# Second query block's maxima moved into the start stage, and x loaded ahead of the values' weights: an attention kernel on one core

## The chip, the core and the metric

The kernel runs on one core of a Trainium2 chip. The core has a matrix engine (TensorE, PE in the profile, with PEld for loading its stationary operand), VectorE (DVE), ScalarE (ACT), GpSimd (POOL), a sync engine (SP) that issues transfers, and 16 DMA engines. Work goes through on-chip memory: SBUF, and eight accumulation banks of 128 x 512 float32 (PSUM) into which TensorE writes. The metric is device time in microseconds (us) of one execution; lower is better.

## What is computed

Two attention layers of 32 heads with 20 features each read the same x (2048 x 640), and a gate mixes their outputs:

```python
def attn(x, wqkv, wo):            # once with A's weights, once with B's
    q, k, v = split(x @ wqkv)     # 32 heads of 20
    p = softmax(q @ k.T * 20 ** -0.5)
    return merge(p @ v) @ wo
g = sigmoid((x * gate_w).sum(-1, keepdims=True))
out = g * attn_A(x) + (1 - g) * attn_B(x)
```

All inputs and the output are float32.

## The kernel before

**Precision.** x and the weights are split in float16 pairs (high and low part), after scaling by a power of two that comes from the largest absolute value of the tensor. `scales` (L171) makes such powers for several tensors at once: a transpose of the column maxima on TensorE (L177), a reduction and some integer arithmetic on VectorE (L166 to L187), two tiny products that spread the result to all partitions (L194), and a copy (L197). It is a generator that marks with `PRODUCT` the places where TensorE is used. A projection takes three products per chunk of 128 features (high-high, high-low, low-high), so fifteen for 640 features.

**Tiling.** Heads go in groups of four (`g`, 16 groups over both layers), queries in blocks of 512 (`qb`, four), keys in chunks of 512 (`ch`, four) or tiles of 128. A step `G` of the main loop handles two key tiles of one (g, qb): eight score products (L670), eight exponentials on ScalarE (L673), two groups of value products accumulated in `acc` (L688), and, where one is due, a slice of a coming projection (L405). There are 512 steps, eight for each (g, qb).

**Row maxima.** Softmax needs the maximum of each query's scores before its exponentials. It is made in a pass of its own. A unit `u` of that pass is one query tile of 128 and two heads; eight units make one (g, qb). For each of the four key chunks and two heads, `max_mm` (L596) makes one product (L612) in a bank and evicts it. Plain eviction is a reduction on VectorE (L623). With `two`, chunks are taken in pairs: the first product uses the difference of two key chunks (tiles `KD`), ScalarE takes its relu into `rl` (L616), and VectorE adds the second chunk's product and reduces in one instruction (L620), which replaces one of two reductions by a relu. Before the change `two` holds for both pairs of chunks in block 0 (u < 8), for the first pair with both heads in the rest of group 0, and for the first pair of one head later. `finish_max` (L627) then brings the eight units' maxima through VectorE, GpSimd and a small round trip over DRAM (`m_scr`, L644 and L648, issued on SP) into extra rows of the queries' tile.

**Order.** It is written out by hand; every engine runs its own instructions in the order in which they are emitted, and waits in that order. `take` (L133) picks one of seven banks by the kernel's own clock estimate.

- The start stage (from L863): loads on SP, on ScalarE's and on GpSimd's queue; absolute maxima (`largest`); one chain of `scales` for five tensors; transposes of x (L900) with their splits on ScalarE and VectorE (L904, L905); projection of the first group's keys and some query features (`a_chunk`), of the remaining query features (`r_chunk`, L947), each spread to its rows by small DMAs on SP and GpSimd alternately (L451, L453); the key differences (`differences_of`, GpSimd, L496 to L500).
- The ramp (L990): for each half (chunk pair) and each of the eight units of block 0, four products of maxima, then `go_on` with the rest of the first projections (`rest`: three remainder chunks, then the sixteen tiles of the values' projection) for 1.3 us of the kernel's own clock. Then `finish_max` for block 0, with `rest` going on.
- The main loop (L1125 on): in each step `next_maxima` (L1114) hands out the coming units' chunks: four a step when the unit lies fourteen steps ahead, at 1.5 times that pace while it is nearer (`RAMP`), none when it would be fifteen or more ahead (`LEAD`).

Of the kernel before, what the change touches and what calls it, by code (L numbers as in the profile page):

```python
# [11 lines left out]
F32 = mybir.dt.float32  # L12
I32 = mybir.dt.int32
AF = mybir.ActivationFunctionType
OP = mybir.AluOpType
AX = mybir.AxisListType
# [3 lines left out]
P = 128  # L20
S = 2048
D = 640
# [32 lines left out]
        "X m0 m1 e0 m1 e0 e1 V e1 e0 m1 m0 V e1 m0 m1 m0 e0 e1 X")  # L55
LATE = "e0 e1 e0 e1 V X e0 e1 e0 e1 V"
RAMP = 1.5
BETWEEN = 1.3
NB = 7

T_SCORE, T_MODE, T_VALUES, T_READY = 0.217, 0.1, 0.85, 0.39
# [9 lines left out]
def kernel(  # L71
# [57 lines left out]
    block_end = [0.0, None]  # L129
    free_at, held = [0.0] * NB, set()  # L130
    now = [-1]

    def take():  # L133

# [19 lines left out]
    def tick_block(cost, ready=0.0):  # L154

        begin = block_end[0] if now[0] < 0 and block_end[1] == rows_free else max(rows_free) + T_MODE
        clock["pe"] = max(begin, ready)
        rows_free[:] = [clock["pe"] + cost + T_MODE] * 2
        block_end[:] = [clock["pe"] + cost, list(rows_free)]
        clock["done"] = clock["pe"] + cost + T_READY - T_MODE  # L160
# [10 lines left out]
    def scales(maxima, n, then):  # L171

        for _ in range(REST):
            yield
        yield PRODUCT
        i, pt = take()
        nc.tensor.transpose(pt[:n, :P], maxima[:, :n], ident)  # L177
        tick_block(0.1, free_at[i])
        yield
        e = wts.tile([5, 8], F32, name="e", tag="scl", bufs=2)  # L180
        nc.vector.tensor_reduce(e[:n, 0:1], pt[:n, :P], axis=AX.X, op=OP.max)
        give(i, spend("dve", 0.3, clock["done"]))
        spend("dve", 1.0)
        powers(e.bitcast(I32)[:n, :], 1)
        dg = wts.tile([5, 2, 5], F32, name="dg", tag="scd", bufs=2)
        for k in range(2):
            nc.vector.tensor_scalar(dg[:n, k, :n], ident[:n, :n], e[:n, 3 + k:4 + k], None, op0=OP.mult)  # L187
        for _ in range(REST):
            yield
        yield PRODUCT  # L190
        i, pb = take()
        tick_block(0.1, free_at[i])
        for k in range(2):
            nc.tensor.matmul(pb[:, k * n:(k + 1) * n], ones[:n, :], dg[:n, k, :n], start=True, stop=True)  # L194
        yield
        both = wts.tile([P, 10], F32, name="both", tag="scb", bufs=2)
        nc.vector.tensor_copy(both[:, :2 * n], pb[:, :2 * n])  # L197
        give(i, spend("dve", 0.2, clock["done"]))
        then(both[:, :n], both[:, n:2 * n])
# [56 lines left out]
    def largest(dst, src):  # L256
        nc.vector.tensor_reduce(dst, src, axis=AX.XY, op=OP.max,
                                apply_absolute_value=True)
        spend("dve", 0.5)
# [138 lines left out]
    def mms(i, out_ap, pairs, cost):  # L398

        if now[0] >= 0:  # L400
            tick_block(len(pairs) * cost * T_SCORE, free_at[i])
        for k, (a, b) in enumerate(pairs):
            if now[0] < 0:
                tick_block(cost * T_SCORE, free_at[i])
            nc.tensor.matmul(out_ap, a, b, start=(k == 0), stop=(k == len(pairs) - 1))  # L405
            if now[0] < 0:
                yield

    def turns(n):

# [32 lines left out]
    def run(gen):  # L443
        for _ in gen:
            pass
# [145 lines left out]

    def max_parts(g, qb):
        m = mparts[g, qb] = wts.tile([P, 2, 2, 4, 4], F32, name="mpart", tag="mpart", bufs=2)
        nc.gpsimd.memset(m[:, :, 0:1 if g else 2, :, 0] if g or qb else m, LOW)

    def max_mm(u, ch, heads=(0, 1)):  # L596

        g, qb, i = unit_of(u)
        pair, t = divmod(i, 4)
        if (g, qb) not in mparts:
            max_parts(g, qb)
        q0 = qb * QB + t * P
        for j in heads:
            two = u < NS or ch < 2 and (j == 0 or g == 0)
            i, pt = take()
            ready = tick_score(j, i)
            r = slice(64 * j, 64 * j + 60)  # L610
            k = KD[g % 2 if ch == 0 else 1][r, pair] if two and ch % 2 == 0 else KT[g % 2][r, pair, ch * QB:(ch + 1) * QB]
            nc.tensor.matmul(pt, QT[g % 2][r, pair, q0:q0 + P], k, start=True, stop=True)  # L612
            m = mparts[g, qb][:, pair, j, t, ch:ch + 1]
            if two and ch % 2 == 0:
                relus[u, j] = start.tile([P, QB], F32, name="rl0", bufs=4) if u < NS else work.tile([P, QB], F32, name="rl", bufs=2)
                nc.scalar.activation(relus[u, j], pt, AF.Relu)  # L616
                back = relu_at[u, j] = spend("act", T_EXP, ready)
            elif two:
                rl = relus.pop((u, j))
                nc.vector.tensor_tensor_reduce(rl, pt, rl, 1.0, LOW, OP.add, OP.max, m)  # L620
                back = spend("dve", T_MAX, max(ready, relu_at.pop((u, j))))
            else:
                nc.vector.tensor_reduce(m, pt, axis=AX.X, op=OP.max)  # L623
                back = spend("dve", T_MAX, ready)
            give(i, back)
# [244 lines left out]
    w_t = wqkv[0].rearrange("(c p) f -> p c f", p=P)  # L870
    for part in range(2):
        nc.sync.dma_start(ws[:, part], w_t[:, :, part * D:part * D + 320])
    nc.sync.dma_start(wv[:, :, :160], w_t[:, :, 2 * D:2 * D + 160])
    for i in range(0, NT, 2):
        nc.sync.dma_start(xs[:, i:i + 2, :], x_t[:, i:i + 2, :])
    nc.scalar.dma_start(wv[:, :, 160], gate_w.rearrange("(c p) -> p c", p=P))
    mrow = wts.tile([P, S], F16, name="mrow", tag="cq", bufs=2)[:4]
    nc.gpsimd.memset(mrow, MS)
    for i in range(2):
        for j in range(2):  # L880
            nc.gpsimd.dma_start(KT[i][64 * j + 60:64 * j + 64], mrow.unsqueeze(1).to_broadcast([4, 2, S]))
    for i in range(2):
        nc.gpsimd.memset(V[i][:, :, :, DH:VW], 1.0)
    xm = start.tile([P, 8], F32, name="xm")
    wm = start.tile([P, 5], F32, name="wm")
    for part in range(2):
        largest(wm[:, part:part + 1], ws[:, part])
    largest(wm[:, 2:3], wv[:, :, :160])
    largest(wm[:, 3:4], wv[:, :, 160:161])
    for i in range(8):  # L890
        largest(xm[:, i:i + 1], xs[:, 2 * i:2 * i + 2, :])
    nc.vector.tensor_reduce(wm[:, 4:5], xm, axis=AX.X, op=OP.max)

    def turn(j0, c):

# [13 lines left out]
    def turns_of(j0, cs=range(NC)):  # L909
        for c in cs:  # L910
            turn(j0, c)()
            yield

    max_parts(0, 0)
    load, split_next = weights_a(1)
    load()
    drains = [turn(0, c) for c in range(NC)] + [turn(4, 0)]
    found = []
    run(scales(wm, 5, lambda r, inv: found.extend((r, inv))))
    r, inv = found  # L920
    r_x = r[:, 4:5]
    hi, lo = blk["a", 0] = block_tiles("a")
    split_now(ws[:, 1, :, 0:GF], r[:, 1:2], hi[:, :, 0:GF], lo[:, :, 0:GF])
    split_now(ws[:, 0, :, 0:48], r[:, 0:1], hi[:, :, GF:P], lo[:, :, GF:P])
    for f in drains:
# [5 lines left out]
    nc.gpsimd.tensor_copy(hi.rearrange("p c (j f) -> p c j f", j=4), w_r)  # L931
    nc.gpsimd.tensor_tensor(lo.rearrange("p c (j f) -> p c j f", j=4), w_r, hi.rearrange("p c (j f) -> p c j f", j=4),
                            op=OP.subtract)
    nc.vector.tensor_copy(inv_x, inv[:, 4:5])
    halves = []
    both = cycle((nc.sync, nc.gpsimd))

    def a_chunk(ch):
        if ch % 2 == 0:
            halves.append(half_tiles(0))  # L940
        n = slice((ch % 2) * QB, (ch % 2 + 1) * QB)
        hl = halves[ch // 2][:, :, n]
        yield from project_chunk(blk["a", 0], hl[:, 0], hl[:, 1], ch)
        for pair in range(2):
            run(spread(0, hl, ch * QB, QB, q=(0,) if ch == pair == 0 else (), k=(pair,), queues=both))

    def r_chunk(ch, pairs):  # L947
        yield from project_r(0, ch)
        n = slice((ch % 2) * QB, (ch % 2 + 1) * QB)
        run(spread(0, halves[ch // 2][:, :, n], ch * QB, QB, q=pairs, k=(), queues=both))  # L950
        spread_done.add((0, ch))

    def beside(gen, n, other):

        for k, _ in enumerate(gen):
            if k % n == n - 1:
                next(other, None)
        run(other)
# [10 lines left out]
    beside(a_chunk(1), 3, turns_of(8))  # L969
    differences_of(0, KD[0])  # L970
    beside(a_chunk(2), 3, turns_of(12))
    run(r_chunk(0, (1,)))
    run(a_chunk(3))
    differences_of(1, KD[1])
    hi, lo = v_tiles(0)
    split_now(wv[:, :, :160], r[:, 2:3], hi[:, :, :160], lo[:, :, :160])
    split_now(wv[:, :, 160:161], r[:, 3:4], hi[:, :, 160:161], lo[:, :, 160:161])
    nc.vector.tensor_scalar(inv_g, inv[:, 3:4], inv_x, -1.0, op0=OP.mult, op1=OP.mult)
    set_qk(0, r[:, 0:2], inv[:, 0:2])
    set_v(0, r[:, 2:3], inv[:, 2:3])  # L980
    split_next()
    rest = series(*(r_chunk(ch, (0, 1)) for ch in (1, 2, 3)), *(project_v(0, j) for j in range(0, NT, 2)))

    def go_on(us):

        end = clock["pe"] + us
        while clock["pe"] < end and next(rest, PRODUCT) is not PRODUCT:
            pass

    for half in range(2):  # L990
        for u in range(NS):
            for ch in (2 * half, 2 * half + 1):
                max_mm(u, ch, (1, 0))
            go_on(BETWEEN)
    while side:
        advance()
    chain = finish_max(0, 0)
    for _ in chain:
        go_on(0.5)
    run(rest)  # L1000
    start_stack.close()

# [101 lines left out]
        except StopIteration:  # L1104
            current.clear()

    maxima = [(u, ch) for u in range(NS, STEPS) for ch in ORDER]
    debt = [0.0]

    def spread_of(u):  # L1110
# [106 lines left out]
```

## Time and profile before

| what | value |
|---|---|
| three runs | 2784.59, 2784.76, 2785.21 us; median 2784.76 us |
| the profiled execution's own time | 2784.79 us |
| its span, first to last instruction | 2782.9 us |
| mean granted TensorE clock | 0.996 |
| VectorE, ScalarE, GpSimd busy | 2447.3, 2522.9, 673.0 us |
| bytes read from and written to HBM | 55.53 MB, 31.86 MB |

The profile comes from one execution. Its views: the page (busy shares, the chain of work that ended last, the costliest groups of instructions); the timeline (instructions in order of time, merged where alike); the chain of waits in order of time; and tables of busy time by stretch of the span. A matmul's busy time contains its pipeline, so a busy PE is not PE at its peak. In a group "x560 | 377.0, 677" is 560 instructions, 377.0 us busy together, 677 ns each from start to end; overlapping ones count once in the first number. "[0.69 <-DMA ws]" is idle time of the engine before a row, and what ended it. A few matmul records can be missing.

### The profile page before, as it was taken

The page shows a single profiled execution, that of the slowest core. Times are in us where ns is not written, and L with a number is a line of the kernel's source. Part 1 is how long each engine was busy: PE and PEld are TensorE (multiplying, and loading weights), DVE is VectorE, ACT ScalarE, POOL GpSimd, SP SyncE. Part 2 cuts the span into 40 slices and gives each one's busy share as a digit, 9 for nine tenths or more (in the row PEclk, how much of TensorE's full clock was granted, in tenths as well). Part 3 has the DMA queues.
Part 4 walks back from the last instruction along what each step waited for, and adds up shares of the span by engine and source line. Part 5 has one row for each costly group of instructions (what it writes and reads, how often), then busy time and mean ns, then how long its engine had stood idle before and what let it go on. Part 6 is the DMA issues. An engine that isn't in the chain of part 4 may idle for free.

```text
span 2782.9 us, 61802 instructions
## 1 busy us (share of the span) xinstructions
PE 2731.9 (98%) x23062; PEld 933.6 (34%) x23062; DVE 2447.3 (88%) x4759; ACT 2522.9 (91%) x5106; POOL 673.0 (24%) x914
## 2 busy tenths in 40 slices
PE   6999999999999999999999999999999999999998
PEld 3533332333333332333333333333333333322222
DVE  6789999889999999888888998989988898999982
ACT  3799999999999999999999999999999999989987
POOL 5322122312122421321221212222342202100111
PEclk9999999999999999999999999999999999999999
DMA  4021102001120212202012231221201112132112
GB/s 135 21 57 26 31 10 47 8 17 30 24 50 23 49 36 63 47 8 61 21 32 74 60 78 30 51 59 51 64 19 42 28 51 62 32 88 55 42 47 75
DMA packets 176397, 125.54 MB, mean 45 GB/s; under 512 B 105184, under 2 KB 145944, under 8 KB 176096
## 3 DMA queue, kind: packets, MB, share of 16 engines
q1 hardware_dynamic: 173552, 119.99, 17.1%
q8 instruction: 180, 2.95, 0.5%
q0 software_dynamic: 1600, 0.96, 0.2%
q14 instruction: 121, 0.99, 0.1%
q10 hardware_dynamic: 944, 0.66, 0.1%
HBM read 55.53 MB, written 31.86 MB: 31 GB/s over the span
## 4 chain that ended last, share of the span: by engine, by line
PE 91%; DVE 5%; ACT 1%; DMA 1%; POOL 1%; issue 1%; SPq 0%; POOLq 0%; DVEq 0%; ACTq 0%
PE acc L688 35%; PE bank L405 19%; PE bank L612 19%; PE bank L670 18%; DVE mpart L623 3%; ACT pt L673 1%; DVE rl L620 1%; DMA xs<-in_A_x_dram 0%; ACT rl L616 0%; PE bank L851 0%; DMA wv<-in_A_wqkv_dram 0%; DVE ot L774 0%; PE bank L900 0%; DMA wstage<-in_A_wqkv_dram 0%; DMA m_scr<-m4r 0%
## 5 line engine op out<-in xcount | busy, mean ns | idle before, releaser
L673 ACT ACTIVATE pt<-bank 128x512 f32<-128x512 f32 x4096 | 2168.1, 612 | 154.2 <-PE bank L670 95.3
L623 DVE TENSOR_REDUCE mpart<-bank 128x1 f32<-128x512 f32 x2976 | 1862.7, 681 | 217.1 <-PE bank L612 116.8
L688 PE MATMUL acc<-pt,v 128*21 128x512 f32 x8192 | 1081.7, 600 | 1.7 <-DVE ot L774 1.6
L670 PE MATMUL bank<-qt,kt 64*128 64x512 f16 x4096 | 1052.0, 380 | 7.6 <-DVE mpart L623 3.9
L612 PE MATMUL bank<-kt,qt 60*128 60x512 f16 x3536 | 1018.8, 380 | 5.1 <-ACT pt L673 1.7
L612 PEld LDWEIGHTS <-qt 60*128 60x128 f16 x4096 | 237.8, 94 | 864.7 <-issue 805.3
L620 DVE CUSTOM_DVE_ANT_0 rl<-bank,rl 128x512 f32<-128x512 f32 x560 | 377.0, 677 | 16.7 <-ACT rl L616 10.4
L616 ACT ACTIVATE rl<-bank 128x512 f32<-128x512 f32 x560 | 329.8, 595 | 10.1 <-PE bank L612 8.5
L670 PEld LDWEIGHTS <-kt 64*128 64x128 f16 x4096 | 235.6, 94 | 240.1 <-issue 123.2
L688 PEld LDWEIGHTS acc<-pt,v 128*21 128x21 f32 x8192 | 143.0, 99 | 436.8 <-issue 429.4
L405 PE MATMUL bank<-xx,wbh 128*128 128x168 f16 (+3 forms) x2400 | 286.8, 239 | 2.7 <-ACT xx L904 1.9
L405 PE MATMUL bank<-xx,wbl 128*128 128x168 f16 (+3 forms) x1200 | 256.3, 237 | 0.0
L782 POOL TENSOR_TENSOR ot<-ot,sq 128x512 f32<-128x512 f32 x63 | 66.1, 1049 | 773.8 <-DVE sq L779 753.1
L405 PEld LDWEIGHTS <-wbh 128*128 128x128 f16 x2400 | 189.7, 98 | 109.7 <-issue 102.4
L612 PE MATMUL bank<-kd,qt 60*128 60x512 f16 x560 | 203.3, 379 | 1.8 <-DMA kd<-dd 1.2
L434 POOL CAST cq<-fs 128x512 f16<-128x512 f32 x60 | 36.7, 612 | 515.6 <-ACT fs L432 507.9
L405 PE MATMUL bank<-woh,o_in 128*128 128x320 f16 (+1 forms) x640 | 155.7, 301 | 0.0
L405 PE MATMUL bank<-wvh,xx 128*128 128x160 f16 (+1 forms) x1280 | 155.2, 234 | 0.1
L405 PEld LDWEIGHTS <-xx 128*128 128x128 f16 x1920 | 131.5, 97 | 52.2 <-issue 49.1
L405 PE MATMUL bank<-wvl,xx 128*128 128x160 f16 (+1 forms) x640 | 137.3, 231 | 0.5 <-POOL wvl L345 0.5
L405 PEld LDWEIGHTS <-wbl 128*128 128x128 f16 x1200 | 117.5, 98 | 4.3 <-issue 0.8
L405 PEld LDWEIGHTS <-o_in 128*128 128x128 f16 (+1 forms) x960 | 80.7, 97 | 91.8 <-issue 64.6
(139 smaller groups left out, 1237.5 us busy)
## 6 DMA issues: line engine op xcount, KB each, us to landing
y_scr<-y_out SPq DMA_DIRECT2D x48, 320.0 KB
y_out<-y_scr SPq DMA_DIRECT2D x32, 320.0 KB
kt<-cq SPq DMA_DIRECT2D x120, 80.0 KB
o_scr<-on SPq DMA_DIRECT2D x240, 40.0 KB
o_in<-o_scr SPq DMA_DIRECT2D x64, 96.0 KB
kt<-cq SPq DMA_DIRECT2D x136, 40.0 KB
wstage<-in_B_wqkv_dram SPq DMA_DIRECT2D x13, 400.0 KB
xs<-in_A_x_dram SPq DMA_DIRECT2D x8, 640.0 KB
```

The source lines that it names most:

```text
L405: nc.tensor.matmul(out_ap, a, b, start=(k == 0), stop=(k == len(pairs) - 1))
L434: nc.gpsimd.tensor_copy(hi, f)
L612: nc.tensor.matmul(pt, QT[g % 2][r, pair, q0:q0 + P], k, start=True, stop=True)
L616: nc.scalar.activation(relus[u, j], pt, AF.Relu)
L620: nc.vector.tensor_tensor_reduce(rl, pt, rl, 1.0, LOW, OP.add, OP.max, m)
L623: nc.vector.tensor_reduce(m, pt, axis=AX.X, op=OP.max)
L670: nc.tensor.matmul(et, KT[g % 2][r, pair, kt * P:(kt + 1) * P], QT[g % 2][r, pair, qb * QB:(qb + 1) * QB], start=True, stop=True)
L673: nc.scalar.activation(pt, et, AF.Exp, scale=factor(g // 4))
L688: nc.tensor.matmul(acc[32 * h:32 * h + VW, :], V[(g // 2) % 2][:, kt, (g % 2) * GH + h, :], ptiles.pop((G, kk, h)), start=(kt == 0), stop= ...
L782: nc.gpsimd.tensor_tensor(t3, t3, sq.unsqueeze(2).to_broadcast([P, 16, 32]), op=OP.mult)
```

## The change

It has four parts. SP issues the eight loads of x before the load of the values' weights; the gate's column (ScalarE's queue) and the four loads of constant rows into the keys' tiles (GpSimd's queue) are issued later, after the first splits. The values' and the gate's weights get their largest values and a chain of `scales` of their own, after the third chunk's projection and around the fourth; the first chain is left with three tensors. The ramp covers two blocks (`AHEAD`): 32 rounds of four products, with `rest` shared out evenly by a count of the estimated projection time emitted (`streamed`), and `finish_max` emitted at each block's end; block 1 is evicted with `two` in both halves, as block 0 is. The main loop's list of maxima starts at unit 16 instead of 8.

```diff
--- before.py
+++ after.py
@@ -55,7 +55,7 @@
         "X m0 m1 e0 m1 e0 e1 V e1 e0 m1 m0 V e1 m0 m1 m0 e0 e1 X")
 LATE = "e0 e1 e0 e1 V X e0 e1 e0 e1 V"
 RAMP = 1.5
-BETWEEN = 1.3
+AHEAD = 2
 NB = 7
 
 T_SCORE, T_MODE, T_VALUES, T_READY = 0.217, 0.1, 0.85, 0.39
@@ -129,6 +129,7 @@
     block_end = [0.0, None]
     free_at, held = [0.0] * NB, set()
     now = [-1]
+    streamed = [0.0]
 
     def take():
 
@@ -402,9 +403,10 @@
         for k, (a, b) in enumerate(pairs):
             if now[0] < 0:
                 tick_block(cost * T_SCORE, free_at[i])
+                streamed[0] += cost * T_SCORE
             nc.tensor.matmul(out_ap, a, b, start=(k == 0), stop=(k == len(pairs) - 1))
             if now[0] < 0:
-                yield
+                yield True
 
     def turns(n):
 
@@ -591,7 +593,7 @@
 
     def max_parts(g, qb):
         m = mparts[g, qb] = wts.tile([P, 2, 2, 4, 4], F32, name="mpart", tag="mpart", bufs=2)
-        nc.gpsimd.memset(m[:, :, 0:1 if g else 2, :, 0] if g or qb else m, LOW)
+        nc.gpsimd.memset(m[:, :, 0:1 if g else 2, :, 0] if g or qb >= AHEAD else m, LOW)
 
     def max_mm(u, ch, heads=(0, 1)):
 
@@ -604,7 +606,7 @@
             max_parts(g, qb)
         q0 = qb * QB + t * P
         for j in heads:
-            two = u < NS or ch < 2 and (j == 0 or g == 0)
+            two = u < AHEAD * NS or ch < 2 and (j == 0 or g == 0)
             i, pt = take()
             ready = tick_score(j, i)
             r = slice(64 * j, 64 * j + 60)
@@ -612,7 +614,7 @@
             nc.tensor.matmul(pt, QT[g % 2][r, pair, q0:q0 + P], k, start=True, stop=True)
             m = mparts[g, qb][:, pair, j, t, ch:ch + 1]
             if two and ch % 2 == 0:
-                relus[u, j] = start.tile([P, QB], F32, name="rl0", bufs=4) if u < NS else work.tile([P, QB], F32, name="rl", bufs=2)
+                relus[u, j] = start.tile([P, QB], F32, name="rl0", bufs=4) if u < AHEAD * NS else work.tile([P, QB], F32, name="rl", bufs=2)
                 nc.scalar.activation(relus[u, j], pt, AF.Relu)
                 back = relu_at[u, j] = spend("act", T_EXP, ready)
             elif two:
@@ -870,26 +872,20 @@
     w_t = wqkv[0].rearrange("(c p) f -> p c f", p=P)
     for part in range(2):
         nc.sync.dma_start(ws[:, part], w_t[:, :, part * D:part * D + 320])
-    nc.sync.dma_start(wv[:, :, :160], w_t[:, :, 2 * D:2 * D + 160])
     for i in range(0, NT, 2):
         nc.sync.dma_start(xs[:, i:i + 2, :], x_t[:, i:i + 2, :])
-    nc.scalar.dma_start(wv[:, :, 160], gate_w.rearrange("(c p) -> p c", p=P))
+    nc.sync.dma_start(wv[:, :, :160], w_t[:, :, 2 * D:2 * D + 160])
     mrow = wts.tile([P, S], F16, name="mrow", tag="cq", bufs=2)[:4]
     nc.gpsimd.memset(mrow, MS)
-    for i in range(2):
-        for j in range(2):
-            nc.gpsimd.dma_start(KT[i][64 * j + 60:64 * j + 64], mrow.unsqueeze(1).to_broadcast([4, 2, S]))
     for i in range(2):
         nc.gpsimd.memset(V[i][:, :, :, DH:VW], 1.0)
     xm = start.tile([P, 8], F32, name="xm")
     wm = start.tile([P, 5], F32, name="wm")
     for part in range(2):
         largest(wm[:, part:part + 1], ws[:, part])
-    largest(wm[:, 2:3], wv[:, :, :160])
-    largest(wm[:, 3:4], wv[:, :, 160:161])
     for i in range(8):
         largest(xm[:, i:i + 1], xs[:, 2 * i:2 * i + 2, :])
-    nc.vector.tensor_reduce(wm[:, 4:5], xm, axis=AX.X, op=OP.max)
+    nc.vector.tensor_reduce(wm[:, 2:3], xm, axis=AX.X, op=OP.max)
 
     def turn(j0, c):
 
@@ -911,14 +907,15 @@
             turn(j0, c)()
             yield
 
-    max_parts(0, 0)
+    for qb in range(AHEAD):
+        max_parts(0, qb)
     load, split_next = weights_a(1)
     load()
     drains = [turn(0, c) for c in range(NC)] + [turn(4, 0)]
     found = []
-    run(scales(wm, 5, lambda r, inv: found.extend((r, inv))))
+    run(scales(wm, 3, lambda r, inv: found.extend((r, inv))))
     r, inv = found
-    r_x = r[:, 4:5]
+    r_x = r[:, 2:3]
     hi, lo = blk["a", 0] = block_tiles("a")
     split_now(ws[:, 1, :, 0:GF], r[:, 1:2], hi[:, :, 0:GF], lo[:, :, 0:GF])
     split_now(ws[:, 0, :, 0:48], r[:, 0:1], hi[:, :, GF:P], lo[:, :, GF:P])
@@ -931,7 +928,11 @@
     nc.gpsimd.tensor_copy(hi.rearrange("p c (j f) -> p c j f", j=4), w_r)
     nc.gpsimd.tensor_tensor(lo.rearrange("p c (j f) -> p c j f", j=4), w_r, hi.rearrange("p c (j f) -> p c j f", j=4),
                             op=OP.subtract)
-    nc.vector.tensor_copy(inv_x, inv[:, 4:5])
+    nc.vector.tensor_copy(inv_x, inv[:, 2:3])
+    nc.scalar.dma_start(wv[:, :, 160], gate_w.rearrange("(c p) -> p c", p=P))
+    for i in range(2):
+        for j in range(2):
+            nc.gpsimd.dma_start(KT[i][64 * j + 60:64 * j + 64], mrow.unsqueeze(1).to_broadcast([4, 2, S]))
     halves = []
     both = cycle((nc.sync, nc.gpsimd))
 
@@ -969,34 +970,49 @@
     beside(a_chunk(1), 3, turns_of(8))
     differences_of(0, KD[0])
     beside(a_chunk(2), 3, turns_of(12))
+    largest(wm[:, 3:4], wv[:, :, :160])
+    largest(wm[:, 4:5], wv[:, :, 160:161])
     run(r_chunk(0, (1,)))
+    of_v = []
+    chain = scales(wm[:, 3:5], 2, lambda r, inv: of_v.extend((r, inv)))
+    while next(chain) is not PRODUCT:
+        pass
+    next(chain)
     run(a_chunk(3))
+    while next(chain) is not PRODUCT:
+        pass
+    next(chain)
+    run(chain)
+    rv, invv = of_v
     differences_of(1, KD[1])
     hi, lo = v_tiles(0)
-    split_now(wv[:, :, :160], r[:, 2:3], hi[:, :, :160], lo[:, :, :160])
-    split_now(wv[:, :, 160:161], r[:, 3:4], hi[:, :, 160:161], lo[:, :, 160:161])
-    nc.vector.tensor_scalar(inv_g, inv[:, 3:4], inv_x, -1.0, op0=OP.mult, op1=OP.mult)
+    split_now(wv[:, :, :160], rv[:, 0:1], hi[:, :, :160], lo[:, :, :160])
+    split_now(wv[:, :, 160:161], rv[:, 1:2], hi[:, :, 160:161], lo[:, :, 160:161])
+    nc.vector.tensor_scalar(inv_g, invv[:, 1:2], inv_x, -1.0, op0=OP.mult, op1=OP.mult)
     set_qk(0, r[:, 0:2], inv[:, 0:2])
-    set_v(0, r[:, 2:3], inv[:, 2:3])
+    set_v(0, rv[:, 0:1], invv[:, 0:1])
     split_next()
     rest = series(*(r_chunk(ch, (0, 1)) for ch in (1, 2, 3)), *(project_v(0, j) for j in range(0, NT, 2)))
 
-    def go_on(us):
-
-        end = clock["pe"] + us
-        while clock["pe"] < end and next(rest, PRODUCT) is not PRODUCT:
+    halves_done = [0]
+    streamed[0] = 0.0
+    whole = (3 * 3 * NC + NT * 3 * NC * 0.33) * T_SCORE
+
+    def go_on(share):
+
+        while streamed[0] < share * whole and next(rest, None) is not None:
             pass
 
-    for half in range(2):
-        for u in range(NS):
-            for ch in (2 * half, 2 * half + 1):
-                max_mm(u, ch, (1, 0))
-            go_on(BETWEEN)
-    while side:
-        advance()
-    chain = finish_max(0, 0)
-    for _ in chain:
-        go_on(0.5)
+    for block in range(AHEAD):
+        for half in range(2):
+            for u in range(block * NS, (block + 1) * NS):
+                for ch in (2 * half, 2 * half + 1):
+                    max_mm(u, ch, (1, 0))
+                halves_done[0] += 1
+                go_on(halves_done[0] / (2 * AHEAD * NS))
+        while side:
+            advance()
+        run(finish_max(0, block))
     run(rest)
     start_stack.close()
 
@@ -1104,7 +1120,7 @@
         except StopIteration:
             current.clear()
 
-    maxima = [(u, ch) for u in range(NS, STEPS) for ch in ORDER]
+    maxima = [(u, ch) for u in range(AHEAD * NS, STEPS) for ch in ORDER]
     debt = [0.0]
 
     def spread_of(u):
```

## Prediction, made before the changed kernel ran

> **What bounds the kernel now.** The page first: what is busy, and the chain that ended last.
>
> ```profile
> span 2782.9 us, 61802 instructions
> PE 2731.9 (98%) x23062; PEld 933.6 (34%) x23062; DVE 2447.3 (88%) x4759; ACT 2522.9 (91%) x5106; POOL 673.0 (24%) x914
> PE 91%; DVE 5%; ACT 1%; DMA 1%; POOL 1%; issue 1%; SPq 0%; POOLq 0%; DVEq 0%; ACTq 0%
> L620 DVE CUSTOM_DVE_ANT_0 rl<-bank,rl 128x512 f32<-128x512 f32 x560 | 377.0, 677 | 16.7 <-ACT rl L616 10.4
> L616 ACT ACTIVATE rl<-bank 128x512 f32<-128x512 f32 x560 | 329.8, 595 | 10.1 <-PE bank L612 8.5
> ```
>
> TensorE stands on nearly the whole chain, but three engines are almost full, so a share says little and I read the stages. The next view splits the span into stretches: length, busy time and instructions of PE, weight loads, DVE, ACT and POOL, granted clock, DMA share, GB/s.
>
> ```profile
> 74.50:86.90 12.40, 12.40 (x138) 8.13 (x137) 9.56 (x28) 10.08 (x29) 11.75 (x21) 1.00 0.24 54
> 86.90:96.20 9.30, 9.30 (x133) 9.24 (x132) 1.93 (x8) 4.58 (x18) 0.90 (x4) 1.00 0.03 4
> ```
>
> The first row is the second half of block 0's maxima, among the first projections; the second is the bare rest of the values' projection. PE is full in both while DVE and ACT have room; in the second DVE is busy for 1.93 us of 9.30. The main loop starts at 98.1 (first exponential). The same split for the exponentials alone (L673, eight to a step) and, in the last two rows, for the maxima's products on PE (L612, busy time of PE and of its weight loads) dates its steps.
>
> ```profile
> 98.10:112.00 13.90, 8.55 (x16) 0.88 0.10 28
> 112.00:189.20 77.20, 51.72 (x96) 1.00 0.16 35
> 189.20:210.50 21.30, 16.93 (x32) 1.00 0.25 63
> 210.50:251.10 40.60, 33.97 (x64) 1.00 0.07 17
> 2704.00:2756.10 52.10, 48.19 (x96) 1.00 0.22 70
> ...
> 112.00:189.20 77.20, 34.38 (x135) 8.34 (x135) 1.00 0.16 35
> 189.20:210.50 21.30, 9.03 (x35) 1.97 (x33) 1.00 0.25 63
> ```
>
> Steps 0 to 13 take 13.90 + 77.20 = 91.1 us, 6.5 each; steps 2 to 13 alone take 6.43, with 135 / 12 = 11.3 products of maxima in each, for the kernel runs 1.5 times the pace to build its lead. Steps 14 to 17 have 35 / 4, about 8, and take 21.30 / 4 = 5.33; the next eight, where one head instead of two is handled with differences, 40.60 / 8 = 5.08. Twelve steps near the end, without any maxima, take 52.10 / 12 = 4.34.
>
> **Part 1, the head: x ahead of the values' weights.** Timeline of the start (start, duration, engine, line; in brackets idle time before it and its releaser), then x's issues on SP and their size from the page, then two stretches with their GB/s last.
>
> ```profile
> 8.66 1.82 DVE L257 TENSOR_REDUCE wm<-ws 128x1 f32<-128x1600 f32 x1 [0.69 <-DMA ws<-in_A_wqkv_dram]
> 12.02 1.05 DVE L257 TENSOR_REDUCE wm<-wv 128x1 f32<-128x800 f32 x2 [1.53 <-DMA wv<-in_A_wqkv_dram]
> 14.43 10.97 DVE L257 TENSOR_REDUCE xm<-xs 128x1 f32<-128x1280 f32 x7 [1.35 <-DMA xs<-in_A_x_dram]
> 25.72 1.49 DVE L257 TENSOR_REDUCE xm<-xs 128x1 f32<-128x1280 f32 x1 [0.32 <-DMA xs<-in_A_x_dram]
> ...
> 2.35 9.99 SPq L875 DMA_DIRECT2D xs<-in_A_x_dram  x8
> ...
> xs<-in_A_x_dram SPq DMA_DIRECT2D x8, 640.0 KB
> ...
> 3.00:6.00 3.00, 0.00 (x0) 0.00 (x0) 0.00 (x0) 0.00 (x0) 2.69 (x6) 1.00 0.91 257
> 6.00:8.00 2.00, 0.00 (x0) 0.00 (x0) 1.82 (x1) 0.00 (x0) 0.70 (x3) 1.00 1.06 385
> 14.00:22.00 8.00, 5.30 (x24) 4.70 (x24) 7.20 (x5) 0.00 (x0) 0.00 (x0) 1.00 1.02 415
> ```
>
> The scales of x need all eight reductions, which end at 25.72 + 1.49 = 27.21. DVE waits 1.53 for wv, reduces it (1.05), and waits 1.35 for x. Without wv ahead, DVE is free at 8.66 + 1.82 = 10.48 and x's first pair, 640 KB at 415 GB/s, is there 1.6 us after the weights, at 10.3. Eight reductions take 10.97 + 1.49 = 12.46, so they end at 22.9: a gain of 4.3. The gate's column and the constant rows no longer compete either: at 385 instead of 257 GB/s from 3 to 6, the weights land (385 - 257) x 3 / 385 = 1.0 us sooner, gain 5.3. If the first pair needs 0.6 us longer, as its landing behind wv suggests (14.43 - 12.02 = 2.4 us after it), the gain is 3.7, and I let it go to 3.3. I take 4.7.
> [...]
>
> **Part 2, what is put back behind x.**
>
> ```profile
> 0.72 0.48 ACTq L876 DMA_DIRECT2D wv<-in_gate_w_dram  x1
> 3.46 2.52 POOL L881 DMA_DIRECT2D kt<-mrow  x4 [0.31 <-POOL mrow L878]
> 27.45 0.38 PE L177 MATMUL bank<-ident,wm 128*5 128x128 f32 x1 [6.78 <-DVE wm L892]
> 29.06 1.01 PE L194 MATMUL bank<-dg,ones 5*128 5x5 f32 x4 [1.23 <-DVE dg L187]
> 35.92 0.69 ACT L904 ACTIVATE xx<-bank,both 128x512 f16<-128x512 f32 x1 [0.55 <-PE bank L900]
> 40.81 0.62 POOL L453 DMA_DIRECT2D kt<-cq  x1 [1.72 <-ACT cq L440]
> 46.81 2.00 POOL L453 DMA_DIRECT2D kt<-cq  x4 [2.77 <-ACT cq L440]
> 58.42 0.50 PE L612 MATMUL bank<-kd,qt 60*128 60x512 f16 x2 [1.22 <-DMA kd<-dd]
> ```
>
> The gate's issue (0.48) falls on ACT into the 0.55 it idles before 35.92. The four constant-row issues take 2.52 of POOL, in front of the first spreads of keys: of those, 1.72 lies in its idle time, 0.8 delays chunk 0's six spreads, and the 2.77 idle before 46.81 swallows that. Without this cover the first maxima, which wait for differences that POOL makes, would be 2.5 later. wv's load and its two reductions (1.05 on DVE) fall in a stretch where PE sets the pace. The chain for the values' scales puts a transpose (0.38) and four tiny products (1.01 at half clock) into PE's order around the last chunk. PE idles 1.22 before the first maxima, waiting for the key differences, so this is hidden but for a few tenths; ACT's split of wv now waits for the chain, so the first relus may come up to 0.9 late. I take 0, bounds 0 and +1.5.
>
> **Part 3, the second block among the projections.** Steps of the chain of waits (start, length, what), then SP's issues of the second key differences.
>
> ```profile
> 55.99 2.30 DMA kd<-dd
> 61.08 1.40 PE bank L405 x6
> 76.27 0.54 PE bank L612 x4
> 76.81 1.17 PE bank L405 x15
> 91.73 3.06 DMA m_scr<-m4r
> 96.62 3.23 DMA wstage<-in_A_wqkv_dram
> ...
> 67.35 3.19 SPq L451 DMA_DIRECT2D kd<-dd  x4
> ```
>
> A unit (one query tile, two chunks, two heads) is four products, two relus and two adding reductions. Its products cost 0.54, and 0.10 more is lost at the switch: 133 products of the values take 9.30, 0.070 each, so fifteen are 1.05 of the 1.17. Likewise six of the remainder's are 1.30 of 1.40, 0.217 each. All projections: 45 x 0.217 + 240 x 0.070 = 26.6. Now: 16 x 0.64 + 26.6 = 36.8 (measured 58.42 to 96.2, 37.8 with its waits). After: 32 x 0.64 + 26.6 = 47.1, that is 1.47 a unit. Added: 10.2.
> Do the others follow in 1.47? DVE has two reductions, 377.0 / 560 = 0.67 each or 1.35; ACT two relus, 329.8 / 560 = 0.59 each or 1.18, plus about 0.8 of a values' drain (4.58 / 9, 0.5 with its gate). By these means, 1.35 and 1.58, ACT would bind. But a lone activation's mean holds its pipeline too, and from 74.5 to 86.9 seven units of 1.71 hold 10.08 of ACT with all drains, 1.4 a unit. That row is nearer to the case and I use it: tight, but under 1.47.
> One wait is new. Half 1 needs the second differences, whose third issue on SP (head 1, pair 0, taken first) starts at 67.35 + 1.6 and lands 2.30 later, at 71.25. Half 1 started after eight units of 1.94 at 74.5; now it is reached at 58.42 + 8 x 1.47 = 70.2: PE waits 1.0. With 0.3 for mismatched drains the stage grows by 11.5; bounds 10.2 and 17, the latter at 1.71 a unit (54.7 - 37.8).
> Block 0's finishing chain lies under block 1. Block 1's now sits at the ramp's end, with SP in order behind it: the wait for m_scr (3.06) holds back the next weights (3.23 to land) by some 7 us, until about 10 after the ramp; their reader is in step 3, some 16 after it. Without that slack DVE would stall, and PE behind it.
>
> **Part 4, the main loop.** It starts with its lead full: no maxima in steps 0 and 1, then four chunks a step from unit 16. Steps 2 to 13 then have the load of steps 14 to 17: 12 x 5.33 = 63.9. For steps 0 and 1 I take 4.5 each (4.34 and a projection more). 72.9 instead of 91.1: gain 18.2. Bounds: 12 x 5.08 + 2 x 4.34 = 69.6, gain 21.5; at 5.7 and 5.0, 78.4, gain 12.7. DVE also loses sixteen reductions there, since block 1 now goes by differences in both halves; this is inside the 18.2.
>
> **The sum**: -4.7 + 0 + 11.5 - 18.2 = -11.4. The profiled execution took 2784.79 (span 2782.9 and 1.9 around it), the runs' median is 2784.76, so 2784.8 - 11.4 = 2773.4.
>
> **Rivals.** (a) The loop's steps fall only half way, to 5.9, because something other than the extra maxima makes the first steps long: 12 x 5.9 + 9 = 79.8, gain 11.3, time 2780.3. For it: steps 0 and 1 have a granted clock of 0.88, which has nothing to do with maxima; against it: from step 2 on it is 1.00, and steps 14 to 17, with more transfers (63 against 35 GB/s), take 5.33.
> (b) The ramp keeps its old 1.71 a unit, as ACT's drains and relus collide: 17 instead of 11.5, time 2778.9. For it: ACT at 1.4 of 1.47; against it: seven banks, four of which a unit takes.
> (c) The slower side: the ramp's units stop overlapping. Then each costs its products, two relus and the last addition, 0.54 + 1.18 + 0.67 = 2.4, and 32 of them take 76.8, 39 more than now: -4.7 + 39 - 18.2, time 2800.9. It decides from 1.9 a unit on ((37.8 + 22.9) / 32). For it: the same banks serve projections; against it: units now run at 1.71 with this chain overlapped.
> (d) x comes no sooner, because SP's issues, not the bytes, pace it: gain 0 in the head, 2778.1. For it: those issues take until 12.3; against it: the last of x lands 13 us later.
> A fifth effect moves little. The clock was granted at half for ten microseconds:
>
> ```profile
> 27.00:32.00 5.00, 1.44 (x6) 1.16 (x7) 1.71 (x11) 1.69 (x4) 0.96 (x1) 0.50 0.00 0
> 32.00:37.00 5.00, 4.80 (x17) 3.05 (x17) 5.00 (x9) 4.05 (x7) 4.76 (x6) 0.50 0.00 0
> ```
>
> With the head moved, this stretch of PE work may be shorter or longer by some microseconds at half speed, +-1 in the time; it is in the range.
>
> **How the numbers follow.** Forecast 0.62, (a) 0.14, (b) 0.11, (c) 0.06, (d) 0.07. The forecast's own bounds, not all at once, give 2768 to 2779; (a) and (b) lift the top. Range 2767 to 2783, leaving out (c), the dearer part of (a) and a larger gain in the loop. A measurement tells 0.2%, 5.6 us: faster is below 2779.2, which takes the forecast, (d) and half of (b), 0.76; within 0.2%, (a) and the rest of (b), 0.18; slower 0.06.
>
> **What would show it.** x's last reduction ending near 22.5; first products of maxima near 53.7, after a short wait of PE for kd; 32 units at about 1.5, with one wait for the second kd; the first exponential near 105; steps 0 and 1 near 4.5 and 2 to 13 near 5.3; from step 14 on the old times, shifted. A ramp beyond 61 us or first steps at 6.4 would make it wrong.

## The result, and the profile after

| | kernel before | changed kernel |
|---|---|---|
| median of 12 runs each, same chip (us) | 2784.85 (2783.57 to 2786.22) | 2778.56 (2777.0 to 2779.84) |
| ratio to before | | 0.9978, 95% interval 0.997 to 0.9986 |
| span of the profiled execution | 2782.9 | 2777.7 |

The change gains 6.3 us, 0.22%, where 11.4 was forecast: the direction was right, the time lies in the range, and the gain is little more than half of the forecast one. The time alone would also fit rival (b), 2778.9, and rival (d), 2778.1; the stages tell them apart. In the changed kernel's listing most lines have moved by one or two: L258 is the reductions (L257 before), L195 the scales' last products (L194), L614 the maxima's products (L612), L407 the projections (L405), L675 the exponentials (L673).

The head, in the timeline of the changed kernel, with the columns as before:

```profile
7.92 1.82 DVE L258 TENSOR_REDUCE wm<-ws 128x1 f32<-128x1600 f32 x1 [0.42 <-DMA ws<-in_A_wqkv_dram]
9.65 12.45 DVE L258 TENSOR_REDUCE xm<-xs 128x1 f32<-128x1280 f32 x8
```

The eight reductions of x run without a gap and end at 9.65 + 12.45 = 22.10 instead of 27.21, so 5.1 earlier; 4.7 was forecast. The second weight tile lands 0.7 sooner (8.66 to 7.92); the DMA engines move 382 GB/s from 3 to 6 us instead of 257, now that neither the gate's column nor the constant rows are under way (which of the two matters was not tried).

The main loop: exponentials by stretch.

```profile
110.40:118.50 8.10, 7.99 (x16) 1.00 0.23 56
118.50:182.80 64.30, 50.46 (x97) 1.00 0.20 45
182.80:203.60 20.80, 16.88 (x32) 1.00 0.22 55
```

Steps 0 and 1 take 8.1 together (9.0 forecast), steps 2 to 13 take 64.3, 5.36 each (63.9 forecast), and steps 14 to 17 take 20.8 where they took 21.3. From 110.4 to 182.8 that is 72.4 instead of 91.1: a gain of 18.7, and 18.2 was forecast. The first exponential, though, comes at 110.5, not near 105. The missing time lies between x's last reduction and there.

Timeline of that place, then two stretches of the changed kernel (length, busy time of PE, weight loads, DVE, ACT and POOL, granted clock, DMA share, GB/s):

```profile
53.65 0.27 DVE L182 TENSOR_REDUCE e<-bank 2x1 f32<-2x128 f32 x1
...
54.75 0.60 PE L195 MATMUL bank<-dg,ones 2*128 2x2 f32 x4 [2.38 <-DVE dg L188]
55.29 0.39 PE L614 MATMUL bank<-kd,qt 60*128 60x512 f16 x2
...
57.27 1.87 PE L407 MATMUL bank<-xx,wbh 128*128 128x512 f16 x4 [1.38 <-ACT rl L618]
...
52.40:55.30 2.90, 0.55 (x6) 0.53 (x7) 1.69 (x8) 0.60 (x1) 2.90 (x6) 1.00 0.38 89
55.30:63.90 8.60, 7.22 (x25) 1.61 (x24) 5.31 (x20) 4.29 (x8) 8.29 (x13) 0.60 0.25 57
```

PE waits 2.38 for VectorE to finish the second scales chain, whose reduction starts only at 53.65, behind the eviction of the fourth chunk. The first product of maxima comes at 55.29, 3.1 earlier than before instead of 5.1. PE then waits 1.38 more for a relu, and in the next 8.6 us the granted clock is 0.60 on the mean; by half microseconds it is 0.50 from 56.5 to 63.0 and 1.00 before 56.0 and from 63.5 on. That is 2 x 0.40 x 8.6 = 6.9 us at half speed, with three units in them. The kernel before has no such stretch at this place, by its row for the first half of the maxima:

```profile
58.40:74.50 16.10, 15.56 (x84) 5.26 (x85) 12.68 (x44) 10.59 (x21) 15.59 (x21) 1.00 0.26 60
```

The chain of waits further on shows the units once they run:

```profile
95.33 0.88 PE bank L407 x11
96.22 0.79 PE bank L614 x4
97.00 0.95 PE bank L407 x12
97.96 0.54 PE bank L614 x4
98.49 0.95 PE bank L407 x12
...
107.20 0.62 PE bank L614 x4
107.81 2.03 PE bank L407 x26
```

Some units' four products take 0.54, as before, others up to 0.79. From the ninth unit (71.5) to the last (107.2) twenty-three units take 35.7, 1.55 each and not 1.47. The last row holds eleven products of the values, to 108.7, and the fifteen of step 0.

### The profile page after: what moved, and what is told of

It is laid out like the page before. It is cut to its first block, busy times and chain, and to the rows that moved or that the text cites. A ratio compares the mean times of both kernels' runs of the same rounds, so it can differ in the third digit from the quotient of the medians.

```text
span 2777.7 us, 61864 instructions
## 1 busy us (share of the span) xinstructions
PE 2732.4 (98%) x23067; PEld 931.6 (34%) x23067; DVE 2441.7 (88%) x4767; ACT 2529.6 (91%) x5122; POOL 671.6 (24%) x914
## 3 DMA queue, kind: packets, MB, share of 16 engines
HBM read 55.53 MB, written 31.86 MB: 31 GB/s over the span
## 4 chain that ended last, share of the span: by engine, by line
PE 93%; DVE 4%; ACT 1%; DMA 1%; issue 0%; POOL 0%; POOLq 0%; SPq 0%; DVEq 0%; ACTq 0%
PE acc L690 35%; PE bank L407 20%; PE bank L614 19%; PE bank L672 18%; DVE mpart L625 3%; ACT pt L675 1%; DMA xs<-in_A_x_dram 0%; DVE rl L622 0%; PE bank L853 0%; PE bank L896 0%; DMA ws<-in_A_wqkv_dram 0%; DVE ot L776 0%; ACT rl L618 0%; DVE es L216 0%; PE bank L828 0%
## 5 line engine op out<-in xcount | busy, mean ns | idle before, releaser
L675 ACT ACTIVATE pt<-bank 128x512 f32<-128x512 f32 x4096 | 2166.8, 615 | 149.5 <-PE bank L672 90.7
L625 DVE TENSOR_REDUCE mpart<-bank 128x1 f32<-128x512 f32 x2944 | 1842.0, 681 | 224.7 <-PE bank L614 123.5
L614 PE MATMUL bank<-kt,qt 60*128 60x512 f16 x3520 | 1014.0, 380 | 4.5 <-DVE mpart L625 1.4
L614 PEld LDWEIGHTS <-qt 60*128 60x128 f16 x4096 | 235.7, 94 | 860.0 <-issue 800.8
L622 DVE CUSTOM_DVE_ANT_0 rl<-bank,rl 128x512 f32<-128x512 f32 x576 | 386.8, 677 | 12.1 <-ACT rl L618 8.0
L618 ACT ACTIVATE rl<-bank 128x512 f32<-128x512 f32 x576 | 337.0, 595 | 11.8 <-PE bank L614 11.2
L407 PE MATMUL bank<-xx,wbh 128*128 128x168 f16 (+3 forms) x2400 | 288.5, 239 | 3.7 <-ACT xx L900 1.9
L407 PE MATMUL bank<-xx,wbl 128*128 128x168 f16 (+3 forms) x1200 | 255.9, 237 | 0.0
L407 PEld LDWEIGHTS <-wbh 128*128 128x128 f16 x2400 | 189.1, 98 | 112.3 <-issue 106.3
L614 PE MATMUL bank<-kd,qt 60*128 60x512 f16 x576 | 204.3, 381 | 0.1
L407 PE MATMUL bank<-wvh,xx 128*128 128x160 f16 (+1 forms) x1280 | 156.0, 234 | 0.0
L407 PE MATMUL bank<-woh,o_in 128*128 128x320 f16 (+1 forms) x640 | 155.7, 301 | 0.0
L407 PEld LDWEIGHTS <-xx 128*128 128x128 f16 x1920 | 131.1, 97 | 57.1 <-issue 54.3
L407 PE MATMUL bank<-wvl,xx 128*128 128x160 f16 (+1 forms) x640 | 137.6, 232 | 0.0
L407 PEld LDWEIGHTS <-wbl 128*128 128x128 f16 x1200 | 117.2, 98 | 4.5 <-issue 1.5
L407 PEld LDWEIGHTS <-o_in 128*128 128x128 f16 (+1 forms) x960 | 80.7, 97 | 91.8 <-issue 64.6
```

What stands on the lines that cost most here:

```text
L675: nc.scalar.activation(pt, et, AF.Exp, scale=factor(g // 4))
```

## The experiments

Times are medians of five or more runs; the kernel before ran beside each group and had 2783.98 (e1 to e4), 2784.36 (e5 to e8) and 2784.08 (e10 to e12). I compare gains against these. Runs of one kernel spread by 0.4 to 3.7 us, so differences below one are not read.

### e1: the chain's VectorE work ahead of the fourth chunk

```diff
     next(chain)
+    next(chain)
     run(a_chunk(3))
```

One more step of the generator emits the reduction and the integer operations before the projection's eviction.

> The changed kernel with one edit: the reduction and the small VectorE operations of the second scales chain are emitted ahead of the fourth chunk's projection instead of behind it. My theory: in the changed kernel PE idles 2.4 us between that projection and the chain's last products only because the chain's VectorE work stands behind the projection's eviction, and this idling is what sends the TensorE clock to half for 6.8 us. Then here the first product of maxima starts near 53.9 instead of 55.3, held only by the key differences' DMA, there is no half clock near 56, the first three units take about 5 us instead of 8.7, and the time falls by 4 to 6, from 2778.6 to about 2773.5. Rival (the half clock comes from the thin first units and the wait for the DMA, whatever the chain does): the first product comes 1.4 earlier, the half clock stays, 2777.2.

2773.64, a gain of 10.3 on before where the changed kernel gained 6.3 (ratio 0.9962, 0.9949 to 0.9976). Timeline, then the stretch of the first two units and the rest:

```profile
51.08 0.60 PE L195 MATMUL bank<-dg,ones 2*128 2x2 f32 x4
52.94 0.50 PE L614 MATMUL bank<-kd,qt 60*128 60x512 f16 x2 [1.25 <-DMA kd<-dd]
...
53.00:57.70 4.70, 4.70 (x18) 1.16 (x19) 3.07 (x12) 2.82 (x6) 4.61 (x9) 0.64 0.32 77
57.70:104.00 46.30, 46.30 (x402) 23.71 (x402) 40.39 (x124) 39.28 (x94) 23.40 (x36) 1.00 0.13 29
```

The last products no longer wait for VectorE, and the first product waits only for the key differences. The half clock is down to 2 x 0.36 x 4.7 = 3.4 us but not gone, against the expectation. The wait of 1.25 that is left does not explain it by its length alone: the kernel before (1.22), e3 (1.19) and e5 (1.31, with the same chain as e1) wait as long at this place and keep the clock at 1.00.
The time follows my theory: every run of e1 (2772.8 to 2774.3) lies below every run of the changed kernel (2777.0 to 2779.8), and the order of the chain costs some 4 us with what follows from it. How much sooner it brings the first product is less sure. In this execution it is 2.4, but 1.2 of that is there ahead of the edit: the fourth chunk's products start at 47.75 instead of 48.98, behind a head with 10.2 us at half clock instead of 13.7. In e5, e6 and e7, which have the same edit, it is 0.4 to 1.3.

### e2: PE kept busy during the wait

```diff
+    def warm(n):
+        for _ in range(n):
+            nc.tensor.transpose(acc[:, :P], xs[:, 0, 0:P], ident)
...
     run(a_chunk(3))
+    warm(20)
```

> The changed kernel with twenty extra transposes into the unused accumulation bank right behind the fourth chunk's projection, so that PE is busy while the second scales chain's VectorE work runs; the order of all else stays. If the half clock near 56 is the price of that idling: the first product stays at about 55.3, the clock stays full, the first three units take about 5.5 us instead of 8.7, time about 2775.5. Rival (the slow first units come from ScalarE's late split of the values' weights and relus, not from the clock): units as slow as before, 2778.6 or a little more.

2774.96 (0.9968, 0.9956 to 0.998), a gain of 9.0.

```profile
52.42 2.35 PE L938 MATMUL acc<-ident,xs 128*128 128x128 f32 x20
55.53 0.39 PE L614 MATMUL bank<-kd,qt 60*128 60x512 f16 x2
...
55.50:61.50 6.00, 4.62 (x27) 1.41 (x27) 4.94 (x18) 4.29 (x8) 5.77 (x8) 1.00 0.28 65
```

Work that computes nothing takes 2.35 us of PE, the first product comes no sooner (55.53), and the kernel is faster by about 2.7 than the changed one, because the clock stays at 1.00. Three units now take 6.0 instead of 8.6. At 1.51 each, the pace of the units behind them, they would take 4.5: of the 4.1 lost there, 2.6 is the clock, and 1.5 stays, which I put down to the relus that wait behind ScalarE's split of the values' weights.
The half clock at this place lasts 6.9 us in the changed kernel and 3.4 in e1, and no single wait of PE there is longer than 2.6 us (e12). With the wait filled, as here, the clock stays at 1.00; why a wait brings the half clock and what sets its length no run here shows.

### e3 and e4: the two halves of the change

e3 has only the second block's maxima; loads, constant rows and one chain for five tensors are as before. e4 has only the loads and the second chain; the ramp and the list of maxima are as before.

```diff
 # e3, against the changed kernel
-    nc.sync.dma_start(wv[:, :, :160], ...)     # behind x
+    nc.sync.dma_start(wv[:, :, :160], ...)     # ahead of x
...
-    run(scales(wm, 3, ...))
+    run(scales(wm, 5, ...))
 # e4, against the changed kernel
-AHEAD = 2
+AHEAD = 1
+BETWEEN = 1.3
...
```

> Only the second block's maxima in the ramp; loads, constant rows and one scales chain for five tensors as in the kernel before. If the parts add up: the head as before (x's last reduction ends at 27.2), the first product at 58.4 as before, no half clock there, the ramp about 49 to 50 us long instead of 53.5, steps 0 to 13 in about 72.4, time 2784.85 + 11.7 - 18.7 = about 2778. Rival (the half clock and the slow first units belong to the denser ramp and not to the moved chain): ramp 53.5 here too, 2781.8.

> Only the loads' order and the second scales chain; the ramp and the main loop's maxima as in the kernel before. If the parts add up: x's last reduction ends near 22.1, the first product near 55.3, a half clock in the first units that costs some 3 to 4, so the 5.1 gained in the head is nearly all given back: 2784.85 - 5.1 + 1.6 + 3.5 = about 2784.5. Rival (the half clock belongs to the denser ramp): 2784.85 - 5.1 + 1.6 = 2781.4.

e3: 2778.54 (0.9979, 0.997 to 0.9988), a gain of 5.4. e4: 2785.68 (1.0006, 0.9997 to 1.0015), no gain and rather a loss of 1.7. Timeline and two stretches of e3, then a stretch of e4:

```profile
71.45 0.47 PEld L614 LDWEIGHTS <-qt 60*128 60x128 f16 x4 [1.87 <-DMA kd<-dd]
71.48 0.50 PE L614 MATMUL bank<-kd,qt 60*128 60x512 f16 x2 [1.40 <-DVE rk L443]
...
57.30:63.80 6.50, 6.28 (x33) 1.89 (x33) 5.72 (x24) 5.12 (x11) 6.33 (x10) 1.00 0.30 68
63.80:108.50 44.70, 43.30 (x381) 22.75 (x381) 38.13 (x116) 36.72 (x89) 21.89 (x35) 1.00 0.12 28
```
```profile
55.10:66.30 11.20, 9.56 (x28) 2.22 (x28) 5.08 (x21) 4.29 (x8) 10.85 (x17) 0.54 0.27 63
```

In e3 the clock is full from the first product on, with the same dense ramp: the half clock belongs to the moved chain and not to the dense ramp. Its ramp lasts 51.2, longer than I expected: its later units take 1.55 too, and before the ninth unit PE idles 1.40. The weight load there waits for the second key differences; the products' own row names VectorE, whose eviction ended last by the profile. That is the wait that the forecast put at 1.0, in the kernel that reaches this place early enough to meet it.
In e4 the clock is at half for 2 x 0.46 x 11.2 = 10.3 us: its units hold six products of the remainder each, all of them stretched (2.68 and 2.42 us for six, 1.40 later). All of the head's 5.1 is given back there and in the chain's wait.

### e5, e6, e7, e8: the units, the bank, the split, the clock in the head

All four are e1 with one edit. e5 leaves out the gate's sixteen exponentials (gates set to 1). e6 adds the accumulation bank, idle until the main loop, as an eighth:

```diff
-    banks = [... for i in range(NB)]
+    banks = [... for i in range(NB)] + [acc]
...
-        i = min((k for k in range(NB) if k not in held), ...)
+        i = min((k for k in range(NB + more[0]) if k not in held), ...)
...
     halves_done = [0]
+    more[0] = 1
...
     run(rest)
+    more[0] = 0
```

e7 emits the values' split behind the third unit. e8 fills PE in the head:

```diff
+    warm(50)
+    first = scales(wm, 3, ...)
...
+    next(first)        # its transpose
+    warm(9)
...
+    next(first)        # its products
+    warm(12)
+    run(first)
```

> The kernel with the chain emitted earlier (e1), and the sixteen exponentials of the gate's column left out (the gates are set to 1 instead, so the mix of the two layers is not computed). It tells what makes a unit of the ramp 1.55 us long instead of the forecast 1.47. Theory A (ScalarE's drains of the values' tiles, two activations each, stand in front of the relus, so the adding reductions and the banks come late): with one activation less per tile, 0.26 us, the units of the values' phase fall to 1.48 to 1.50, the ramp by 1.5 to 2, time about 2772. Theory B (the products simply cost more than 0.64 a unit): units stay at 1.55, 2773.6.

> e1 with an eighth bank during the ramp (the accumulation bank, which is not used before the main loop). If a unit's last two products wait for a bank (0.63 instead of 0.38 for the pair in about every second unit of the values' phase), the units fall to about 1.48, the ramp by about 2, time about 2771.5 to 2772. If ScalarE or VectorE is full at that pace, or the products cost more by themselves, units stay at 1.55 and the time at 2773.6.

> e1 with the split of the values' weights (1.2 us on ScalarE, then GpSimd) emitted behind the third unit of the ramp instead of ahead of the first. If the first two units of e1 are long (2.27 and 2.44) because their relus wait behind that split: they fall to about 1.5 to 1.7, the half clock near 54 gets shorter or goes, time 1.5 to 2.5 below e1, about 2771.5. If the half clock alone makes them long: one unit stays near 2.3 and the gain is under 0.5.

> e1 with 71 extra transposes into the unused accumulation bank, which keep PE busy from the end of x's first transposes (16) until the first splits (27). The clock was at half from 19.7 to 29.9 in e1 and to 32.4 in the changed kernel. If that stretch costs half of the PE work that falls in it: full clock throughout, the first projections' turns at 0.9 instead of 1.7 us, a gain of 1.5 to 2.5, time about 2771.5. If VectorE's and ScalarE's evictions set the pace of the turns, the gain is under 0.5.

e5 2772.62 (0.9958, 0.9944 to 0.9971), e6 2771.52 (0.9953, 0.994 to 0.9967), e7 2775.03 (0.9963, 0.995 to 0.9977), e8 2773.48 (0.9961, 0.9948 to 0.9975); e1 was at 0.9962. The chain of waits of e6:

```profile
92.01 0.54 PE bank L614 x4
92.55 0.39 PE bank L407 x4
92.93 0.57 PE acc L407 x8
93.50 0.54 PE bank L614 x4
94.03 0.60 PE acc L407 x7
94.64 0.35 PE bank L407 x5
94.99 0.54 PE bank L614 x4
```

With eight banks the units' products take 0.54 in all these rows, and from the ninth unit to the last a unit is 1.47, as forecast: the 0.08 that my sum was short of was a wait for a bank. From the fourth unit's start to the last's it is 41.3 us instead of 43.2 in e1, some 2 less. e5 fits this: with one activation less on ScalarE the units are shorter too (1.52), but unevenly; its clock is also full in the ramp, and the gain of about 1 over e1 is at the edge of what can be told. e7 gains nothing that can be told: its first unit is shorter (1.9 instead of 2.3), the second, at half clock, is longer (2.8 instead of 2.4).

e8 puts the clock in the head to 1.00 and yet gains nothing over e1 that can be told. These are the first turns of the changed kernel and of e8, then GpSimd's timeline in e8:

```profile
26.80:32.40 5.60, 5.35 (x19) 3.54 (x19) 5.46 (x9) 4.14 (x7) 5.37 (x6) 0.50 0.02 0
```
```profile
26.80:32.40 5.60, 5.19 (x33) 3.43 (x32) 5.60 (x10) 5.01 (x10) 5.28 (x7) 1.00 0.01 0
...
33.61 2.54 POOL L950 DMA_DIRECT2D kt<-mrow  x4
36.14 0.57 POOL L455 DMA_DIRECT2D kt<-cq  x1
...
38.73 0.51 POOL L455 DMA_DIRECT2D kt<-cq  x1 [0.51 <-DMA kt<-mrow]
40.60 1.51 POOL L455 DMA_DIRECT2D kt<-cq  x3 [1.36 <-DMA kt<-mrow]
```

At full clock PE does 33 products in the 5.6 us instead of 19. What is late next is GpSimd: the constant rows, issued behind its weight splits, hold up its own key spreads, the differences come late, PE waits 2.47 for them, and the first product starts at 52.7, much as in e1 (52.9), again with 3.4 us at half clock behind it. Neither half of my expectation named this. The wait for the rows is no oddity of e8: it is 2.18 us in the changed kernel and 1.53 in e1.

### e10, e11, e12: the rows earlier, all together, and the loads with the chain repaired

e10 is e8 with the four constant-row loads gated on x's last maximum, in GpSimd's idle time:

```diff
+    x_read = start.tile([P, 1], F32, name="x_read")
+    nc.gpsimd.tensor_copy(x_read, xm[:, 7:8])
+    for i in range(2):
+        for j in range(2):
+            nc.gpsimd.dma_start(KT[i][64 * j + 60:64 * j + 64], mrow...)
```

e11 is e10 with the eighth bank; e12 is e4 with e1's edit.

> The kernel with PE kept busy in the head (e8), and the four constant-row loads issued on GpSimd as soon as x's last reduction is done (near 22), into GpSimd's idle time, instead of behind its weight splits (33.7 in e8). In e8 the chain of waits to the first product runs through kt<-mrow: GpSimd's next key spread waited for those rows to land, and the key differences came late. If so: no such wait, the first product near 50.5 instead of 52.7, time about 2771.3. If the spreads were paced by the keys' projection and not by the rows: 52.7 again and 2773.5.

> e10 with the eighth bank in the ramp (as in e6). If the causes found so far add up: first product near 50.5, units of 1.47 to 1.49, ramp about 48 to 49, time about 2769. If the ramp's gain and the head's gain overlap, 2771.

> The loads' order alone (e4, ramp and main loop as in the kernel before) with the second chain's VectorE work emitted ahead of the fourth chunk's projection as in e1. e4 gained 5.1 in the head and ended no faster than the kernel before. If the place of the chain and the half clock that follows it ate the gain: first product near 53 to 54, half clock gone or short, time 2784.0 - 5.1 + 1 to 2 = about 2780.5. If the shorter head is lost for another reason (the later constant rows, the clock in the head): 2784 to 2785 as e4.

e10 2770.25 (0.995, 0.9937 to 0.9964), e11 2768.99 (0.9945, 0.9932 to 0.9959), e12 2780.81 (0.9988, 0.9979 to 0.9997). GpSimd in e10, then the chain of waits and one stretch:

```profile
22.20 0.19 POOL L913 COPY x_read<-xm 128x1 f32<-128x1 f32 x1 [18.33 <-DVE xm L258]
22.44 2.52 POOL L916 DMA_DIRECT2D kt<-mrow  x4
...
33.45 0.62 POOL L455 DMA_DIRECT2D kt<-cq  x1
38.99 1.99 POOL L455 DMA_DIRECT2D kt<-cq  x4 [2.42 <-ACT cq L442]
```
```profile
51.01 1.17 ACT wvh L344 x2
52.18 0.47 ACT rl L618
52.70 0.86 PE bank L614 x4
```
```profile
50.40:98.50 48.10, 47.83 (x412) 24.19 (x413) 43.63 (x140) 41.98 (x99) 28.18 (x44) 1.00 0.16 35
```

The first two fences are e10, the third is e11. In e10 the spreads wait for nothing but the projection, the first product starts at 50.6 after a wait of only 0.49, and the clock stays at 1.00 behind it. Warm head and early rows together are worth 3.5 over e1, where the warm head alone gave nothing; the early rows alone were not run. What stands on the chain next is ScalarE's split of the values' weights. e11 has a ramp of 48.1 at full clock and is the fastest kernel here, 15.1 below the kernel before. e12 gains 3.3 where e4 lost 1.7: the loads' order has a gain, and the place of the chain ate it. Not all of the head's 5.1 is back: PE still waits 2.62 for the key differences, and 3.4 us at half clock follow.

## Why the prediction was right in sign and too large in size

**The head (-4.7)** was right: -5.1 measured. Rival (d) fell: the last reduction ends at 22.1 instead of 27.2.

**What is put back behind x (0, bounds 0 and +1.5)** is the step that failed first. The forecast had the chain "hidden but for a few tenths" in PE's 1.22 of idle time, with only its PE instructions counted. The chain's VectorE part was given no place in VectorE's order; it is emitted behind the fourth chunk's eviction, starts at 53.65, and PE waits for it. Only 3.1 of the head's 5.1 reached the first product, so this step cost 2.0, above its bound. With the chain ahead, 0.4 to 2.4 of that comes back (e1, e5, e6, e7), and then the key differences hold the first product. The constant rows have a part in that: the forecast priced their issue (0.8) and not their landing, for which GpSimd waits 2.18 before a key spread in the changed kernel. Only e10 and e11, with early rows and a warm head, have the first product near 50.5.

**The ramp (+11.5)** measured 53.4 - 37.8 = +15.6, from the first product (55.3) to the end of the values' projection (108.7). The forecast length without double counting is 47.1 + 1.3 = 48.4; adding 11.5 to the measured 37.8 had carried 0.9 of old waits along. Measured on top: 4.1 in the first three units (2.6 clock, 1.5 relus, split by e2), and 43.2 - 41.3 = 1.9 for the bank (e6) where the forecast had 0.3 for mismatched drains. The forecast wait of 1.0 is not seen in the changed kernel, whose slow first units reach the place after the differences have landed; e3 shows it. 48.4 + 4.1 + 1.6 - 1.0 = 53.1, beside 53.4 measured. The clock was named as a fifth effect, but in the head, at +-1; that a new wait would bring it to the ramp was not foreseen. Rival (b) has the right place, ScalarE's drains and the banks, and about a third of its price (1.9 of 5.5); (c) fell, since units overlap as before.

**The main loop (-18.2)** was right: -18.7. Rival (a) fell: without the extra maxima steps 2 to 13 take 5.36 each, where steps 14 to 17 took 5.33 before.

-5.1 + 2.0 + 15.5 - 18.7 = -6.3 from the start to step 14, with 15.5 from the first product to the first exponential (39.7 before, 55.2 after). The runs' medians differ by 6.3 too; the profiled execution's span is 5.2 shorter, and its own time, 2779.56, is among the longest of the twelve. Its last exponentials still come 6.1 sooner (2754.5 and 2760.6); behind them its mean granted clock is 0.83, in the kernel before 0.89.
That the time lies in the range is owed to the range's width, 16 us, and not to the terms: two of the four were right, and the other two missed by 2 and by 4. One sum of chances is off too: faster is 0.62 + 0.07 + 0.055 = 0.745, not 0.76.

## What to carry to other kernels

When a short chain across engines is moved, place every one of its instructions in each engine's order, not only those on the busy engine: here one reduction behind an eviction cost more than the chain's own work. At the place studied here TensorE's waits of 1.96 to 2.62 us were followed by 3.4 to 10.3 us at half clock in six runs (the changed kernel, e4, e6, e7, e8, e12), and such a wait is to be priced with them. Work that computes nothing can fill such a wait, though putting the order right gained no less here (10.3 in e1, 9.0 in e2). An accumulation bank that stands idle in one stage is worth lending to another (some 2 us of the ramp in e6).

## What the hardware showed that was not expected

Twenty useless transposes (2.35 us of PE) made the kernel about 2.7 us faster. The stretches at half clock near the first product, worked out from the granted clock, are 3.4 us in e1, e6, e7, e8 and e12, 6.9 in the changed kernel and 10.3 in e4: one, two and three times 3.4. PE's wait before that product was 1.25 in e1 and 1.96 to 2.62 in the other four; in the changed kernel and e4 it was 2.4, just ahead of the chain's last products, and 1.4 more for a relu. Three waits of 1.19 to 1.31 (the kernel before, e3, e5) brought no half clock, so the length of a wait alone does not decide, and what does is not shown.
